# The first batch's v in a chunk-selecting attention with an MLP: six loads by tile of the sequence in place of sixteen by pair of heads

## The chip, the cores and the metric

The kernel runs on one core of a Trainium2 chip. The metric is the device time of one execution in microseconds (us). The kernel before took 303.6 us, the median of three runs (302.7 to 303.85).

## The reference, cut to what matters

For each of 4 batches and 8 heads, 768 queries attend to 768 keys of 64 elements. The keys stand in 24 chunks of 32. An upper bound of each query's score in each chunk is made from the chunk's smallest and largest key elements, the six causal chunks with the highest bounds are kept, and softmax attention runs over those chunks under the causal mask. The heads are then put side by side to rows of 512, and a layer norm, two matrix products (512 to 2048, ReLU, 2048 to 512) and a residual follow.

```python
k_min, k_max = np.min(k_chunks, axis=3), np.max(k_chunks, axis=3)
ub = np.sum(np.maximum(q[:, :, :, None, :] * k_min[:, :, None, :, :],
                       q[:, :, :, None, :] * k_max[:, :, None, :, :]), axis=-1)
ub = np.where(causal, ub, -1000000000.0)
top_chunks = np.argsort(ub, axis=-1)[..., -top_k:]
...
mask = sel & (pos[:, None] >= pos[None, :])
scores = np.where(mask, scale * np.matmul(q, k.transpose(0, 1, 3, 2)), -1000000000.0)
attn = softmax(scores)
x = np.matmul(attn, v).transpose(0, 2, 1, 3).reshape(B, S, H * D)
out = x + np.maximum(layer_norm(x) * g_ln @ w_ch1, 0.0) @ w_ch2
```

## The kernel before, in words

The work unit is a pair of heads of one batch, called g: 4 batches with 4 pairs each give g = 0 to 15. The sequence is cut into 6 tiles of 128 rows, and into two halves r = 0 and 1 of three tiles. The MLP runs by batch b and half r, on 384 rows at a time.

A pair of heads goes through these functions. `load_qk` brings one half of k and of q, two DMAs each, on the queue of SyncE (L195). `turn` transposes them on TensorE (L223), `q_copy` and `k_copy` write them as fp16 into rings of SBUF, `k_bound` takes the chunks' minima and maxima on VectorE (L268, L269) and leaves them in a tile `kc`. `bounds` (L309 to L326), `select` (L339 to L345), `mask_t` (L354) and `mask_ring` (L359) make the mask. `scores` multiplies q by k on TensorE (L411) and takes the exponential on ScalarE (L417), `diag` cuts the triangle on GpSimd (L424), `values` multiplies by v on TensorE (L437), and `normalise` and `pair_stats` finish the rows on VectorE (L446 to L471). The MLP is `centre`, `x_t` (L497), `rstd` (L491, on GpSimd), `mlp1` (L512, 8 matmuls a call) and `mlp2` (L524, 4 matmuls a call: `mlp2(b, r, i, j)` uses the j-th quarter of w2).

v is loaded by `load_v`, and is cast from fp32 to fp16 by the DMA. A tile `va` holds one pair of heads, with a column of ones behind the 64 elements that sums the weights. For the first batch (g = 0 to 3), `load_v(g, i)` brings half i of the sequence with one DMA for each of the two heads (L214: 128 partitions x 3 tiles x 64 elements), and before the first half a memset of the ones on GpSimd (L212). That gives 16 DMAs, 8 for half 0 and 8 for half 1. For the other batches `load_v(g)` brings a whole pair with one DMA of 128 x 12 x 64 (L204).

The weights of the MLP are loaded in four quarters each, `w1_load` and `w2_load`, also as casting DMAs on GpSimd's queue. A copy of one element ahead of each makes the load wait until a given `kc` is there:

```python
    def w2_load(j, g):
        nc.gpsimd.tensor_copy(w2b[0:1, 4 * j, 0:1], st[g]["kc"][0:1, 0, NCH // 2:NCH // 2 + 1])
        nc.gpsimd.dma_start(w2b[:, 4 * j:4 * j + 4, :], w2_r[:, 4 * j:4 * j + 4, :])
```

The order of the work is a list. Every call is a piece with a due time: the first batch's pieces come from a hand-written sequence (`begin`, with the loads that stand in the table `loads`), the others from formulas. A table `MOVED` adds a small shift to the due time of single calls; then the pieces are sorted and called in that order, and a scheduler keeps the order of each engine's queue, with the first batch's instructions tied to each other (L843 to L862). So GpSimd's queue holds, in order: the constants, the 8 loads of v's half 0, triangles and the 4 loads of w1, the 8 loads of v's half 1, one `rstd`, the 4 loads of w2, and the whole-pair loads of v for g = 4, 5 and on, with triangles among them.

GpSimd's DMAs take eight completion semaphores in turn. A DMA waits until the one eight places before it on this queue has landed; SyncE's DMAs have eight of their own.

Of the kernel before, what the change touches and what calls it, by code (L numbers as in the profile page):

```python
# [19 lines left out]
def kernel(  # L20
# [42 lines left out]
    vap = ctx.enter_context(tc.tile_pool(name="vap", bufs=6))  # L63
# [23 lines left out]
    RT = const.tile([P, S], F16, name="RT", tag="RT")  # L87
    tiny = const.tile([1, 1], F32, name="tiny", tag="tiny")
# [23 lines left out]
    def consts_first():  # L112
# [15 lines left out]
        )  # L128
        nc.vector.memset(hsel, 0.0)
# [69 lines left out]
    def load_v(g, i=None):  # L199
        b, hp = divmod(g, HP)  # L200
        if i is None:
            va = st[g]["va"] = vap.tile([P, 2, NT, VW], F16, name="va", tag="va")
            nc.gpsimd.memset(va[:, :, :, D:D + 1], 1.0)
            nc.gpsimd.dma_start(  # L204
                va[:, :, :, 0:D].rearrange("p h t d -> p (h t) d"),
                v[b, 2 * hp:2 * hp + 2].rearrange("h (t p) d -> p (h t) d", p=P),
            )
            return
        a, z = parts(g)[i]
        if not i:  # L210
            st[g]["va"] = vap.tile([P, 2, NT, VW], F16, name="va", tag="va")
            nc.gpsimd.memset(st[g]["va"][:, :, :, D:D + 1], 1.0)  # L212
        for hh in range(2):
            nc.gpsimd.dma_start(  # L214
                st[g]["va"][:, hh, a:z, 0:D],
                v[b, 2 * hp + hh, a * P:z * P].rearrange("(t p) d -> p t d", p=P),
            )
# [211 lines left out]
    def values(g, r):  # L429
        pt, va = st[g]["pt", r], st[g]["va"]  # L430
# [87 lines left out]
    def mlp2(b, r, i, j):  # L518
# [22 lines left out]
        -3: [(load_v, 0, 0), (load_qk, 0, 1), (load_v, 1, 0)],  # L541
        -2: [(load_v, 2, 0), (load_qk, 1, 1)],
        -1: [(load_v, 3, 0), (load_qk, 2, 1)],
        0: [(load_qk, 3, 1), (w1_load, 0, 2)],
        1: [(w1_load, 1, 3)],
        3: [(w1_load, 2, 3), (w1_load, 3, 3), (load_v, 0, 1)],
        4: [(load_v, 1, 1), (load_v, 2, 1), (load_qk, 4, 0)],
        5: [(w2_load, 0, 0), (w2_load, 1, 0), (load_v, 3, 1), (load_qk, 4, 1)],
# [113 lines left out]
    for b in range(B):  # L662
# [14 lines left out]
        if b == 0:  # L677
# [13 lines left out]
            (): -0.04, (0, 1): -0.009, (0, 2): -0.025, (1,): 0.008, (1, 1): 0.017, (1, 2): 0.017,  # L691
            (2,): 0, (2, 4): 0.006, (2, 5): 0.028, (3,): 0, (3, 1): 0.013, (3, 2): 0.013,
            (4,): -0.048, (5,): 0.008, (5, 5): 0.016, (6,): 0.004, (7,): -0.067, (7, 1): -0.07,
            (8,): -0.436, (9,): -0.025, (9, 5): -0.02, (11,): -0.044, (12,): -0.311, (13,): -0.144,
            (14,): -0.138, (14, 5): -0.134, (15,): -0.21, (15, 4): -0.176, (15, 5): 0,
        },
        "centre": {
            (): 0.008, (0,): -0.017, (0, 1): 0, (0, 1, 0): -0.017, (1,): 0, (1, 0, 2): 0.089,
            (1, 1): 0.033, (1, 1, 1): 0.026,
        },  # L700
        "diag": {
            (): -0.046, (0, 0): 0.016, (0, 1): 0.001, (1, 0): 0.012, (1, 1): -0.067, (2,): 0.003,
            (3, 0): -0.003, (3, 1): 0, (4,): -0.056, (6, 0): -0.044, (6, 1): -0.066, (7, 0): -0.178,
            (7, 1): -0.097, (8, 0): -0.399, (8, 1): -0.6, (9, 0): -0.066, (9, 1): -0.069, (11, 0): 0,
            (11, 1): -0.054, (12, 0): -0.04, (12, 1): 0, (13, 0): -0.146, (13, 1): -0.078,
            (14, 0): 0.003, (14, 1): 0, (15, 0): -0.621,
        },
        "k_bound": {
            (0,): -0.011, (1,): -0.011, (2,): -0.009, (3,): -0.018, (4, 0): 0.007, (4, 1): 0.027,
            (5, 1): 0.022, (6, 0): 0.002, (6, 1): 0.107, (7,): -0.058, (8, 0): -0.331,  # L710
            (8, 1): -0.396, (9, 0): 0.002, (9, 1): 0.065, (11, 0): -0.008, (11, 1): 0.025,
            (12, 0): -0.017, (12, 1): -0.015, (13,): -0.032, (14,): 0.028,
        },
        "k_copy": {
            (0,): -0.004, (1, 0): 0.161, (1, 1): 0.063, (2,): 0.006, (3, 0): -0.011, (3, 1): 0.054,
            (4,): 0.024, (5, 0): 0.511, (5, 1): 0.42, (6,): 0.038, (7, 0): -0.032, (9, 1): 0.023,
            (10,): 0.034, (11, 1): 0.026, (12, 0): 0.938, (12, 1): 0.253, (13, 0): 0.002,
            (13, 1): 0.073, (14,): 0.046, (15,): 0.034,
        },
        "k_diag": {  # L720
            (1,): 0.041, (2, 0): 0.13, (3, 0): 0.033, (3, 1): 0.01, (4,): -0.002, (6,): 0.002,
            (7,): -0.058, (8,): -0.331, (9,): -0.138, (10,): -0.023, (11,): 0.02, (12,): 0.006,
            (13,): -0.032, (14,): -0.108, (15,): -0.076,
        },
        "load_qk": {
            (): -0.438, (0, 0): 0.085, (0, 1): -0.538, (1, 0): 0.034, (1, 1): -0.331, (2, 0): 0,
            (2, 1): -0.329, (3, 0): 0.16, (3, 1): -0.169, (4, 0): -0.33, (4, 1): -0.667,
            (5, 0): -0.543, (5, 1): -1.259, (6, 0): 0.011, (6, 1): -0.111, (7, 0): 0.064,
            (7, 1): 0.002, (8, 0): -0.299, (8, 1): -0.593, (10, 0): 0.015, (10, 1): -0.002,
            (11, 0): -0.01, (11, 1): -0.012, (12, 0): 0.082, (12, 1): 0.004, (13, 0): 0.11,  # L730
            (13, 1): 0.159, (14,): 0.026, (15, 0): 0.317, (15, 1): 0.334,
        },
        "load_v": {
            (2,): -0.087, (3, 0): -0.13, (3, 1): -0.568, (4,): -0.551, (5,): -0.547, (6,): -0.163,
            (7,): 0.215, (8,): -0.124, (9,): 0.342, (12,): 0.279, (13,): 0.241, (14,): 0.301,
            (15,): 0.238,
        },
        "mask_ring": {
            (): 0.017, (0, 0): 0.021, (0, 1): 0, (1, 0): 0.036, (1, 1): -0.009, (2, 0): 0.023,
            (2, 1): 0, (4,): 0.064, (5,): 0.074, (6,): 0.076, (7,): 0.016, (8,): -0.257, (9,): 0.076,  # L740
            (10,): 0.209, (11,): 0.066, (12,): 0.08, (13,): 0.102, (14,): 0.139, (15,): 0.093,
        },
        "mask_t": {
            (): -0.004, (0,): 0, (1, 0): -0.019, (1, 1): -0.002, (2,): 0.002, (4,): -0.016,
            (5,): -0.068, (7,): -0.064, (8,): -0.337, (10,): -0.001, (11,): -0.014, (12,): 0.002,
            (13,): -0.082, (14,): 0, (15,): -0.006,
        },
        "mlp1": {
            (0, 0, 2): -0.016, (0, 0, 6): 0.106, (0, 0, 10): 0.098, (0, 0, 14): 0.069,
            (0, 1): -0.023, (0, 1, 0): 0, (0, 1, 2): 0.016, (0, 1, 14): 0.055, (1,): -0.026,  # L750
            (1, 0, 0): 0.016, (1, 0, 2): 0.016, (1, 0, 4): 0.028, (1, 0, 8): -0.014,
            (1, 1, 0): -0.036, (1, 1, 4): -0.178, (1, 1, 10): 0, (1, 1, 14): -0.001, (2,): -0.294,
            (2, 0, 6): -0.616, (2, 0, 12): -0.277, (2, 1, 2): -0.353, (2, 1, 6): -0.28,
            (2, 1, 10): -0.228, (3,): 0.103, (3, 0, 2): 0, (3, 0, 4): 0, (3, 0, 12): 0,
            (3, 0, 14): 0, (3, 1, 0): 0, (3, 1, 4): 0.108, (3, 1, 6): 0, (3, 1, 14): 0.094,
        },
        "mlp2": {
            (): -0.156, (0, 0, 1, 0): -0.071, (0, 0, 1, 3): 0, (0, 0, 2, 0): -0.051, (0, 1): -0.154,
            (0, 1, 0): -0.156, (0, 1, 0, 0): -0.184, (0, 1, 0, 3): -0.145, (0, 1, 1, 0): -0.156,
            (0, 1, 1, 1): 0.152, (0, 1, 2, 0): -0.132, (1,): -0.157, (1, 0, 0, 1): 0,  # L760
            (1, 0, 1, 3): -0.053, (1, 1): -0.138, (1, 1, 0): -0.182, (1, 1, 0, 3): -0.138,
            (1, 1, 2, 2): -0.182, (1, 1, 2, 3): -0.182, (2,): -0.298, (2, 0, 0): -0.323,
            (2, 0, 0, 1): -0.46, (2, 0, 0, 3): -0.305, (2, 0, 1, 0): -0.323, (2, 0, 2, 2): -0.34,
            (2, 0, 2, 3): -0.34, (2, 1): 0, (2, 1, 0, 0): -0.34, (2, 1, 0, 1): -0.18,
            (2, 1, 0, 2): -0.323, (2, 1, 0, 3): -0.298, (2, 1, 1, 0): -0.267, (2, 1, 1, 1): -0.298,
            (2, 1, 1, 2): -0.423, (2, 1, 1, 3): -0.568, (3,): -0.233, (3, 0, 0): 0,
            (3, 0, 0, 2): -0.124, (3, 0, 0, 3): -0.233, (3, 0, 2): -0.332, (3, 1, 0, 0): -0.332,
            (3, 1, 0, 1): -0.374, (3, 1, 1, 1): -0.263, (3, 1, 1, 2): -0.443, (3, 1, 1, 3): -0.009,
            (3, 1, 2, 0): -0.009, (3, 1, 2, 1): 0.115, (3, 1, 2, 2): -0.224, (3, 1, 2, 3): -0.152,
        },  # L770
        "normalise": {
            (1, 0): -0.008, (2,): 0.002, (3,): -0.004, (4, 0): -0.01, (4, 1): -0.002, (6,): 0.002,
            (7,): -0.058, (8,): -0.331, (9,): 0.002, (12,): 0.006, (13,): -0.032, (14, 0): 0.065,
            (14, 1): 0.028,
# [10 lines left out]
            (13, 1): 0.028, (14,): 0.079, (15, 1): -0.015,  # L785
        },
        "q_relu": {
            (4,): -0.097, (5,): 0.065, (6,): 0.052, (7,): 0.041, (8,): -0.224, (9,): 0.084,
            (11,): 0.063, (12,): -0.045, (13,): 0.022,
        },  # L790
        "q_ring": {
# [99 lines left out]
```

## Time and profile before

| what | value |
|---|---|
| runs | 303.6, 302.7 and 303.85 us |
| the profiled execution, its time | 303.4 us |
| its span, first to last instruction | 301.4 us |
| TensorE clock granted | 0.997 of full |
| TensorE's tail, from its last matmul to the end of the span | 4.5 us |
| read from HBM, written to it | 27.27 MB, 6.29 MB |
| packets of GpSimd's DMA queue (q0), of SyncE's (q1) | 29,248 and 60,416 |

A packet here is what one DMA engine moves in one go: one run of 64 elements for q, k and v, one run of 512 elements (1024 bytes as fp16) for the weights. "Landing" is the time from issue to the completion of a DMA. "Idle before" is the idle time of an engine just before a group, with what ended it. A wait names the waiting engine and line, and behind the arrow who released it.

### The profile page before, as it was taken

To read this page: it belongs to the slowest core of one execution; us is meant where nothing else is said; L and a number is where in the kernel's file an instruction comes from. 1 tells how busy PE (TensorE), PEld (TensorE's weight loads), DVE (VectorE), ACT (ScalarE), POOL (GpSimd) and SP (SyncE) were. 2 spreads that over 40 slices of the span, in tenths; PEclk is the share of its full clock that TensorE was granted. 3 is DMA by queue.
4 is the path that set the end of the run, shared out by engine and by line. 5 is a ranking of instruction groups with operands and counts; after the bars stand their busy time and mean duration, and the time that the engine had idled before them with its cause. 6 is when DMAs were issued, how large, how long until landed. Compare 5 with 4: busy or idle time off the path is not lost.

```text
span 301.4 us, 7194 instructions
## 1 busy us (share of the span) xinstructions
PE 288.2 (96%) x2753; PEld 195.4 (65%) x2753; DVE 190.8 (63%) x654; ACT 183.5 (61%) x274; POOL 91.1 (30%) x162
## 2 busy tenths in 40 slices
PE   7887998999999999999999999999999999999993
PEld 3874766765777676777767667766666555555541
DVE  7888655679998788999577768577262282011011
ACT  3983997664788667778665674848368524423310
POOL 9559383152444412733230411223021120000000
PEclk9999999999999999999999999999999999999998
DMA  7999999999659649679572210113010110010111
GB/s 131 208 210 198 180 199 196 164 193 204 149 135 187 124 72 165 110 143 148 88 132 62 78 46 2 41 49 90 35 37 0 37 37 35 35 37 35 70 37 71
DMA packets 90226, 31.41 MB, mean 104 GB/s; under 512 B 78416, under 2 KB 87120, under 8 KB 90192
## 3 DMA queue, kind: packets, MB, share of 16 engines
q1 hardware_dynamic: 60416, 23.61, 33.8%
q0 software_dynamic: 29248, 7.34, 24.8%
q8 instruction: 22, 0.36, 0.5%
q14 instruction: 12, 0.10, 0.1%
q10 hardware_dynamic: 528, 0.00, 0.1%
HBM read 27.27 MB, written 6.29 MB: 111 GB/s over the span
## 4 chain that ended last, share of the span: by engine, by line
PE 75%; DMA 8%; POOL 7%; issue 4%; DVE 4%; ACT 1%; POOLq 0%; ACTq 0%
PE yp L524 24%; PE mm L512 24%; PE mm L411 10%; PE sm L437 6%; PE tr L223 4%; DMA w2b<-in_moe_w_ch_dram 4%; DMA w1b<-in_moe_w_ch_dram 4%; PE ub L326 3%; POOL va L214 2%; PE trh L497 1%; POOL pt L424 1%; PE trh L354 1%; DVE xc L482 1%; ACT pt L417 1%; POOL rstd L491 1%
## 5 line engine op out<-in xcount | busy, mean ns | idle before, releaser
L417 ACT ACTIVATE pt<-mm 128x1024 f16<-128x1024 f32 (+1 forms) x96 | 86.2, 918 | 25.7 <-PE mm L411 25.3
L524 PE MATMUL yp<-w2b,hT 128*128 128x512 f16 x384 | 95.9, 379 | 1.5 <-DMA w2b<-in_moe_w_ch_dram 1.5
L512 PE MATMUL mm<-xT,w1b 128*128 128x384 f16 x512 | 94.3, 326 | 0.0
L516 ACT ACTIVATE hT<-mm 128x768 f16<-128x768 f32 x64 | 51.9, 813 | 49.1 <-PE mm L512 48.8
L512 PEld LDWEIGHTS <-w1b 128*128 128x128 f16 x512 | 48.9, 98 | 29.9 <-issue 0.2
L524 PEld LDWEIGHTS <-hT 128*128 128x128 f16 x384 | 36.4, 98 | 31.8
L424 POOL TENSOR_SCALAR_AFFINE_SELECT pt<-pt 128x768 f16<-128x768 f16 x32 | 28.8, 899 | 89.1 <-ACT pt L417 89.1
L530 DVE SCALAR_TENSOR_TENSOR ot<-yp,rstd,x 128x512 f32<-128x512 f32 x24 | 17.9, 746 | 45.9 <-PE yp L524 45.9
L411 PE MATMUL mm<-QA,KA 128*128 128x128 f16 (+2 forms) x224 | 34.5, 245 | 1.0 <-ACT hT L516 0.5
L411 PE MATMUL mm<-QB,KB 128*128 128x128 f16 (+2 forms) x224 | 34.2, 246 | 0.0
L437 PEld LDWEIGHTS <-pt 128*128 128x128 f16 x672 | 24.6, 98 | 5.6 <-POOL pt L424 1.8
L437 PE MATMUL sm<-va,pt 128*128 128x65 f16 x672 | 26.5, 193 | 1.4 <-POOL pt L424 1.3
L411 PEld LDWEIGHTS <-KA 128*128 128x128 f16 x224 | 17.9, 99 | 8.1 <-issue 2.3
L471 DVE BATCH_NORM_STATS2 bst<-x 128x6 f32<-128x128 f32 x96 | 21.9, 282 | 0.8
L268 DVE TENSOR_REDUCE kc<-tr 128x12 f32<-128x384 f32 x32 | 17.6, 549 | 6.6 <-PE tr L223 4.9
L411 PEld LDWEIGHTS <-KB 128*128 128x128 f16 x224 | 18.0, 98 | 3.5 <-issue 0.8
L446 DVE RECIPROCAL rden<-sm 128x6 f32<-128x6 f32 x32 | 6.1, 191 | 19.7 <-PE sm L437 19.6
L447 DVE TENSOR_TENSOR x<-sm,rden 128x384 f32<-128x384 f32 x32 | 17.8, 557 | 1.0
L223 PE MATMUL tr<-ident_f,qn 128*128 128x128 f32 x96 | 16.2, 278 | 1.3 <-DMA qn<-in_q_dram 1.3
L269 DVE TENSOR_REDUCE kc<-tr 128x12 f32<-128x384 f32 x32 | 17.5, 547 | 0.0
L279 ACT CAST kh<-tr 128x384 f16<-128x384 f32 x24 | 11.6, 484 | 9.2 <-DMA KB<-kh 3.2
L223 PE MATMUL tr<-ident_f,kn 128*128 128x128 f32 x96 | 16.2, 278 | 0.0
(87 smaller groups left out, 354.2 us busy)
## 6 DMA issues: line engine op xcount, KB each, us to landing
kn<-in_k_dram SPq DMA_DIRECT2D x64, 96.0 KB, 3.3
qn<-in_q_dram SPq DMA_DIRECT2D x64, 96.0 KB, 3.7
out_dram<-ot SPq DMA_DIRECT2D x24, 256.0 KB, 2.1
va<-in_v_dram POOLq DMA_DIRECT2D x12, 192.0 KB, 5.5
w1b<-in_moe_w_ch_dram POOLq DMA_DIRECT2D x4, 512.0 KB, 7.7
w2b<-in_moe_w_ch_dram POOLq DMA_DIRECT2D x4, 512.0 KB, 11.2
KA<-kh SPq DMA_DIRECT2D x24, 48.0 KB, 2.1
KB<-kh SPq DMA_DIRECT2D x24, 48.0 KB, 2.0
```

Of the source, the lines that this page charges most:

```text
L223: nc.tensor.transpose(pst[:, t * P:(t + 1) * P], src[:, t], ident_f)
L268: nc.vector.tensor_reduce(kc[:, 0, n], view, axis=AX.X, op=ALU.min)
L411: nc.tensor.matmul(sc[:, hh, o:o + w * P], ks[:, t * P:(t + 1) * P], qs[:, s * P:(s + w) * P], start=True, stop=True,)
L417: nc.scalar.activation(pt[:, n0:n1].rearrange("p n h x -> p h n x"), sc[:, :, 0:o].rearrange("p h (n x) -> p h n x", x=P), ACTF.Exp, scale ...
L424: nc.gpsimd.affine_select(out=dv, in_=dv, compare_op=ALU.is_ge, fill=0.0, base=0, pattern=[[0, 2 * TR], [1, P]], channel_multiplier=-1,)
L437: nc.tensor.matmul(pv[:, hh, s2, :], pt[:, where[t, s], hh, :], va[:, hh, t, 0:D + 1], start=(t == 0), stop=(t == s),)
L447: nc.vector.tensor_tensor(xh(b, r)[:, :, 2 * hp:2 * hp + 2, :].rearrange("p s h d -> p h s d"), pv[:, :, :, 0:D], rden.to_broadcast([P, 2, ...
L471: nc.vector.bn_stats(h["st"][:, i, hp], xh(b, r)[:, i, 2 * hp:2 * hp + 2].rearrange("p h d -> p (h d)"),)
L512: nc.tensor.matmul(hp_[:, i, 0:TR * P], w1b[:, kt, (m + i) * P:(m + i + 1) * P], h["xT"][:, kt], start=(kt == 0), stop=(kt == KT1 - 1),)
L516: nc.scalar.activation(h["hT"][:, m:m + 2], hp_[:, :, 0:TR * P], ACTF.Relu, scale=HS)
L524: nc.tensor.matmul(yp, h["hT"][:, kt, i * P:(i + 1) * P], w2b[:, kt, :], start=(kt == 0), stop=(kt == KT2 - 1),)
L530: nc.vector.scalar_tensor_tensor(ot, yp, h["rstd"][:, i:i + 1], xh(b, r)[:, i].rearrange("p h d -> p (h d)"), op0=ALU.mult, op1=ALU.add,)
```

## The change

v of the first batch gets a tile of its own, `v_first`, for all eight heads and the six tiles of the sequence. `load_v(0, i)` now brings tile i of the sequence for all heads, with one DMA of 128 x 8 x 64. Six calls take the place of 16 DMAs. The ones are set by one memset on VectorE at the start, in place of four on GpSimd. `values` takes its pair out of `v_first` when g is under 4. The pool of `va` has one buffer fewer (5). The table `loads` places the calls: tiles 0 and 1 at step -3, tile 2 at step -2, tile 3 at step 3, tiles 4 and 5 at step 4.

With it the table `MOVED` is another one throughout. On the queues its effects are these. On GpSimd, the whole-pair load of g = 4 (memset and DMA) now stands between the second and the third load of w2, where before all four loads of w2 came first; `w2_load` has entries of its own. On TensorE, all 12 transposes of the first `x_t` stand behind the transposes of q of g = 0, half 1, where before three stood ahead of it and three behind the first matmuls of `mlp1`; further on, calls of `mlp1`, `mlp2`, `scores` and `turn` change places with their neighbours. The number of matmuls of each kind is the same. SyncE's queue has the same order through the first 68 rows of its listing, and swaps a few later.

```diff
-    vap = ctx.enter_context(tc.tile_pool(name="vap", bufs=6))
+    vap = ctx.enter_context(tc.tile_pool(name="vap", bufs=5))
...
+    v_first = const.tile([P, H, NT, VW], F16, name="v_first", tag="v_first")
...
+        nc.vector.memset(v_first[:, :, :, D:D + 1], 1.0)
         nc.vector.memset(hsel, 0.0)
...
-        a, z = parts(g)[i]
-        if not i:
-            st[g]["va"] = vap.tile([P, 2, NT, VW], F16, name="va", tag="va")
-            nc.gpsimd.memset(st[g]["va"][:, :, :, D:D + 1], 1.0)
-        for hh in range(2):
-            nc.gpsimd.dma_start(
-                st[g]["va"][:, hh, a:z, 0:D],
-                v[b, 2 * hp + hh, a * P:z * P].rearrange("(t p) d -> p t d", p=P),
-            )
+        nc.gpsimd.dma_start(v_first[:, :, i, 0:D], v[0, :, i * P:(i + 1) * P].rearrange("h p d -> p h d"))
...
-        pt, va = st[g]["pt", r], st[g]["va"]
+        pt = st[g]["pt", r]
+        va = v_first[:, 2 * g:2 * g + 2] if g < HP else st[g]["va"]
...
-        -3: [(load_v, 0, 0), (load_qk, 0, 1), (load_v, 1, 0)],
-        -2: [(load_v, 2, 0), (load_qk, 1, 1)],
-        -1: [(load_v, 3, 0), (load_qk, 2, 1)],
+        -3: [(load_v, 0, 0), (load_qk, 0, 1), (load_v, 0, 1)],
+        -2: [(load_v, 0, 2), (load_qk, 1, 1)],
+        -1: [(load_qk, 2, 1)],
         0: [(load_qk, 3, 1), (w1_load, 0, 2)],
         1: [(w1_load, 1, 3)],
-        3: [(w1_load, 2, 3), (w1_load, 3, 3), (load_v, 0, 1)],
-        4: [(load_v, 1, 1), (load_v, 2, 1), (load_qk, 4, 0)],
-        5: [(w2_load, 0, 0), (w2_load, 1, 0), (load_v, 3, 1), (load_qk, 4, 1)],
+        3: [(w1_load, 2, 3), (w1_load, 3, 3), (load_v, 0, 3)],
+        4: [(load_v, 0, 4), (load_v, 0, 5), (load_qk, 4, 0)],
+        5: [(w2_load, 0, 0), (w2_load, 1, 0), (load_qk, 4, 1)],
         6: [(w2_load, 2, 1), (w2_load, 3, 1)],
...
         "load_v": {
-            (2,): -0.087, (3, 0): -0.13, (3, 1): -0.568, (4,): -0.551, (5,): -0.547, (6,): -0.163,
...
+            (0, 0): -0.129, (0, 1): -0.083, (4,): -0.551, (5,): -0.582, (6,): -0.163, (7,): 0.215,
...
+        "w2_load": {
+            (0,): 0.265, (1,): 0.256, (2,): 0.189, (3,): 0.183,
+        },
```

## The prediction, made before the changed kernel was run

> **What bounds the kernel now.** I read the busy times first, then the busy time by stage, what TensorE waits for, the chain of waits up to that wait, and last the DMA view of that stage. The page:
>
> ```profile
> PE 288.2 (96%) x2753; PEld 195.4 (65%) x2753; DVE 190.8 (63%) x654; ACT 183.5 (61%) x274; POOL 91.1 (30%) x162
> ```
>
> TensorE is the bound; GpSimd, whose instructions the change removes, is busy for 30%. By stage (span, TensorE busy, and so on):
>
> ```profile
> 0.00:28.00 28.00, 22.72 (x209) 16.97 (x210) 22.45 (x93) 17.65 (x35) 20.14 (x41) 1.00 1.18 187
> 28.00:49.50 21.50, 20.63 (x193) 15.98 (x191) 13.68 (x43) 20.78 (x40) 12.17 (x22) 1.00 1.35 191
> 49.50:53.00 3.50, 1.96 (x11) 0.84 (x10) 1.66 (x11) 1.73 (x2) 1.48 (x2) 1.00 1.22 196
> 53.00:70.00 17.00, 17.00 (x207) 12.37 (x207) 12.72 (x46) 11.67 (x15) 5.31 (x10) 1.00 1.60 189
> ```
>
> TensorE's 13.2 us of idle lie in few places: 5.3 before 28, 0.9 to 49.5, 1.5 to 53, only 1.0 from 53 to 296.9 (0 + 0.58 + 0.46 in the same table), and a tail of 4.5. So after 53 us the end moves by what the start loses or gains. The one long wait near that border, from the view of waits:
>
> ```profile
> PE yp L524 <- DMA w2b<-in_moe_w_ch_dram: 1.5, 1, 1.5
> ```
>
> The ninth matmul of `mlp2` needs the third quarter of w2. The first eight end at 51.42 and it starts at 52.96. The chain of waits into it:
>
> ```profile
> 36.02 0.74 POOL va L214
> ...
> 40.66 12.26 DMA w2b<-in_moe_w_ch_dram
> ...
> 52.96 0.38 PE yp L524
> ```
>
> and GpSimd's timeline ahead of it (start, duration, idle before in brackets):
>
> ```profile
> 25.87 4.64 POOL L214 DMA_DIRECT2D va<-in_v_dram  x6
> 32.34 0.76 POOL L214 DMA_DIRECT2D va<-in_v_dram  x1 [1.82 <-DMA w1b<-in_moe_w_ch_dram]
> 36.02 0.77 POOL L214 DMA_DIRECT2D va<-in_v_dram  x1 [2.93 <-DMA w1b<-in_moe_w_ch_dram]
> ```
>
> Read alone, this says that eight loads of v keep GpSimd until 36.8 and w2 goes out late. The DMA view for 28 to 53 us says otherwise (packets, MB, share of 16 engines), as do the times to landing, each asked in a window of its own: second and third quarter of w2, then v of g = 4 and of g = 5:
>
> ```profile
> q0 software_dynamic: 6054, 3.23, 92.0%
> q1 hardware_dynamic: 6098, 1.50, 40.5%
> ```
>
> ```profile
> w2b<-in_moe_w_ch_dram POOLq DMA_DIRECT2D x1, 512.0 KB, 10.1
> ...
> w2b<-in_moe_w_ch_dram POOLq DMA_DIRECT2D x1, 512.0 KB, 12.3
> ...
> va<-in_v_dram POOLq DMA_DIRECT2D x1, 192.0 KB, 17.4
> ...
> va<-in_v_dram POOLq DMA_DIRECT2D x1, 192.0 KB, 18.0
> ```
>
> GpSimd's DMA queue (q0) is backlogged throughout. Issue plus landing gives one file: w1's last quarter 35.7, the eight loads of v 36.7 to 42.3, w2's quarters 46.2, 49.5, 53.0 and 56.2, then v of g = 4 at 60.1, g = 5 at 62.6. From one to the next: 6.6 us for v's 3,072 packets, 3.9 for the first quarter, 3.3 for each later one, 3.9 and 2.5 for 1,536 packets of v. What comes when depends on the place in this file, not on when GpSimd issues.
>
> [...]
>
> **The change part by part.**
>
> *Issues and memsets.* 16 issues x 0.772 us (median of L214) and 4 memsets x 0.169 leave GpSimd: 13.0 us. Six issues come. Their cost isn't shown; per DMA it lies between 0.77 (384 packets) and 1.06 (1,536, L204), for 1,024 packets I take 0.92 by the straight line, 5.5 in all. In the first half 3.9 us are saved (6.7 - 2.8), but after its constants GpSimd waits until 14.77 for ScalarE's exponential (3.16 us), so they vanish. In the second half the saving reaches only the issue of w2, which queues behind the same packets. Worth 0.
>
> *Packets.* v has 3,072 packets per half before and after. What a run of 8 heads in place of 3 tiles does to a packet is not shown: I take the same 6.6 us, and 5.0 as the low bound, twice the pace of g = 5.
>
> *First half of v.* Its first use is at 16.77 us. Before, the last of the 8 DMAs landed at 14.8 (issue 9.95, 4.8 to landing). Now three are issued by about 7 us, so they aren't later unless each packet is slower. They meet the loads of q and k that TensorE waits for (0.7 us at 7.25, 0.6 at 10.5). From 5 to 14 us q0 moved 3,197 packets, already behind its issues, so q and k lose 0 to 0.5 us. Whatever moves before 49 us is swallowed by the wait for w2 anyway.
>
> *The memset on VectorE* delays the start by 0.06 to 0.33 us (the memsets of L129 and L136), taken as 0.1; *the transposes of `x_t`* behind those of q may win the 0.3 and 0.16 us of idle on L497. Both end in the same wait: 0.
>
> *Eight semaphores.* Before, the last two loads of v waited for w1 (1.8 and 2.9 us). With ten DMAs fewer the loads of half 1 wait for old loads only; the third and fourth load of w2 wait for w1's last two quarters (about 32 and 36 us). Queued behind them on GpSimd is the triangle of g = 0, half 1, run at 43.7: not late. Worth 0 while the queue is backlogged.
>
> *v of g = 4 ahead of w2's third quarter.* This is the step that costs. On GpSimd it is a memset (0.17) and an issue (1.04), hidden. In the file it is 1,536 packets: 3.9 us by its own landing, 2.5 by that of g = 5; I take 3.2. So w2's third quarter lands at 53.0 + 3.2 = 56.2 where TensorE wants it at about 51.4. TensorE waits 4.7 us in place of 1.5. [...] The fourth quarter is as late (59.4), and its first user moves from 59.78 to about 63: no second wait.
>
> *The rest of `MOVED`.* The matmuls are the same, and from 53 us on TensorE has 1.0 us of idle to lose: -0.5 to +1, taken as 0.
>
> *Sum.* 303.4 (the profiled execution: span 301.4 and 2.0 around it) + 3.2 = 306.6. The median of the runs is 303.6, 0.2 above it, within their spread. Own range: +2.5 - 0.5 to +3.9 + 1, so 305.4 to 308.3[...].
>
> **The rivals.** *The eight heads pack better.* If v runs at the pace of g = 5, half 1 takes 5.0 in place of 6.6 and g = 4 takes 2.5: +0.9, so 304.3, no change that can be measured. For it: g = 5 to 7 landed 2.5 to 2.8 us apart. Against it: v of g = 4, with runs of 12, took 3.9.
>
> *The chain of waits is right, and the wait goes.* The other side: GpSimd is free at 28.7 in place of 36.8, w2 goes out some 8 us earlier, and if the file moves with the issues the wait of 1.5 us at L524 ends: 303.4 - 1.5 = 301.9, and no more, since the remaining idle isn't touched. It decides once w2's third quarter lands before 51.4, which with g = 4 ahead of it needs 4.8 us out of the file. Against it: landings every 3.3 us with no gap.
>
> *The new order costs by itself*, without w2: TensorE gets new gaps after 53 us, by 2 us or more: 305.5. For it: VectorE and ScalarE are busy for 9.4 and 9.1 of 10 us around 80 to 90. Against it: the order there changes by neighbours only.
>
> **How the numbers follow.** Forecast 0.58, better packing 0.21, the wait gone 0.15, new order 0.06. About 0.5% (1.5 us) is what a measurement can tell from no change here. The first and last are slower by more; the second is within; the third is faster: 0.64, 0.21, 0.15. The range runs from 302.2, which cuts off most of the third, to 308.6, which takes in the forecast's high end.
>
> **What would show it.** Right: the idle before L524 at w2 grows to 4 to 5.5 us, v of g = 4 lands before w2's third quarter, and busy TensorE time stays at 288. Wrong: that wait is under 2 us; or w2's third quarter lands by 52; or GpSimd's earlier freedom shows in landings before 45 us. Wrong too: a wait on `va` or on q in the first 28 us that reaches past 50.

## The result, and the profile after

The changed kernel takes 311.13 us (median, 310.61 to 312.94), the kernel before beside it 303.55 us: a ratio of 1.0265, 95% interval 1.0218 to 1.0312. That is 7.6 us slower, where 3 were predicted, and above the predicted range (302.2 to 308.6). The profiled execution took 310.83 us, its span is 308.8 (before: 303.4 and 301.4).

The page of the kernel after, busy times and granted clock:

```profile
PE 293.7 (95%) x2753; PEld 199.9 (65%) x2753; DVE 191.2 (62%) x655; ACT 184.0 (60%) x274; POOL 83.4 (27%) x148
...
PEclk9959999999999999999999999999999999999999
```

TensorE runs the same 2,753 matmuls but is busy 5.5 us longer. The work is the same, so the clock must have fallen, and the digit 5 in the third slice of `PEclk` says where: about 15 to 23 us. The stages (span, TensorE busy, ..., and third from the end the granted clock):

```profile
0.00:28.00 28.00, 23.33 (x169) 18.74 (x170) 17.30 (x76) 16.21 (x33) 11.66 (x24) 0.82 1.01 162
28.00:49.50 21.50, 18.46 (x160) 13.40 (x158) 15.02 (x54) 15.77 (x30) 12.28 (x22) 1.00 1.34 184
49.50:53.00 3.50, 3.43 (x28) 2.63 (x27) 1.39 (x5) 3.46 (x7) 3.50 (x7) 1.00 1.45 172
53.00:70.00 17.00, 15.55 (x176) 10.87 (x176) 10.83 (x39) 11.85 (x17) 3.54 (x7) 1.00 1.54 178
```

By 28 us, 169 matmuls are done in place of 209, in more busy time. The loss is at the very start, not near 53 us. TensorE's timeline there shows what came ahead of the clock's fall; first after, then before:

```profile
9.99 0.52 PE L218 MATMUL tr<-ident_f,kn 128*128 128x128 f32 x3 [0.26 <-DMA kn<-in_k_dram]
12.55 0.52 PE L218 MATMUL tr<-ident_f,qn 128*128 128x128 f32 x3 [2.04 <-DMA qn<-in_q_dram]
```

```profile
10.50 0.52 PE L223 MATMUL tr<-ident_f,qn 128*128 128x128 f32 x3 [0.62 <-DMA qn<-in_q_dram]
```

The transposes of q of g = 2 start 2.05 us later, after a wait of 2.04 us in place of 0.62. Then the clock, in stretches cut at its changes:

```profile
10.54:13.95 3.41, 1.40 (x15) 1.39 (x15) 2.02 (x7) 1.68 (x5) 0.00 (x0) 1.00 1.35 213
13.95:24.19 10.24, 10.24 (x71) 9.34 (x71) 4.40 (x22) 7.16 (x14) 2.78 (x5) 0.50 0.83 153
24.19:28.00 3.81, 3.41 (x49) 2.76 (x48) 3.19 (x15) 1.89 (x3) 1.62 (x2) 1.00 1.24 218
```

For 10.24 us TensorE works without a gap at a granted clock of 0.50, which by that share costs 5.1 us. The delay of 2.05 and these 5.1 make 7.2; some small waits vanish, and the first matmul of `mlp1` starts at 34.84 us in place of 28.38: +6.5.

Why was q late? SyncE issued it at the same time in both kernels: its last DMA goes out at 6.61 us, but takes 5.81 us to land (chain of waits, after) in place of 3.8 (DMA view, before):

```profile
6.61 5.81 DMA qn<-in_q_dram
```

```profile
qn<-in_q_dram SPq DMA_DIRECT2D x1, 96.0 KB, 3.8
```

So it was the transfer that took longer. Packets of GpSimd's queue (q0, here v) and of SyncE's (q1, q and k) from 7 to 11 us, after and then before:

```profile
q0 software_dynamic: 2468, 0.31, 121.1%
q1 hardware_dynamic: 1434, 0.35, 55.0%
```

```profile
q0 software_dynamic: 1629, 0.20, 79.3%
q1 hardware_dynamic: 2380, 0.58, 75.5%
```

The sum is the same (3,902 and 4,009), but v moved 839 more packets and q and k 946 fewer. GpSimd issued v's 3,072 packets within 2.9 us (4.22 to 7.1) in place of 6.5 us (4.22 to 10.73). After, then before:

```profile
4.22 2.88 POOL L212 DMA_DIRECT2D v_first<-in_v_dram  x3
```

```profile
4.22 1.75 POOL L214 DMA_DIRECT2D va<-in_v_dram  x2
...
9.19 1.55 POOL L214 DMA_DIRECT2D va<-in_v_dram  x2
```

By 7.1 us GpSimd's queue had moved 298 packets, before the change 475. An estimate from these numbers: some 2,800 packets of v were issued and not yet moved at that moment, against 700 to 1,100 before.

And the step that was forecast? The chain of waits and the waits at w2's third quarter:

```profile
39.83 19.43 DMA w2b<-in_moe_w_ch_dram
59.30 0.38 PE yp L520
```

```profile
PE yp L520 <- DMA w2b<-in_moe_w_ch_dram: 1.3, 1, 1.3
```

v of g = 4, issued at 38.34, lands 17.8 us later, at 56.1, and w2's third quarter at 59.3: v of g = 4 does stand ahead of it. But TensorE waits 1.3 us, not 4.7, since it was itself 6.5 us late. The ninth matmul of `mlp2` starts at 59.30 in place of 52.96, +6.3; the remaining 1.1 of the 7.4 us by which the span grew come later.

### The profile page after: what moved, and what is told of

The parts are those of the page before. It is cut to its first block, busy times and chain, and to the rows that moved or that the text cites. A ratio compares the mean times of both kernels' runs of the same rounds, so it can differ in the third digit from the quotient of the medians.

```text
span 308.8 us, 7189 instructions
## 1 busy us (share of the span) xinstructions
PE 293.7 (95%) x2753; PEld 199.9 (65%) x2753; DVE 191.2 (62%) x655; ACT 184.0 (60%) x274; POOL 83.4 (27%) x148
## 4 chain that ended last, share of the span: by engine, by line
PE 70%; DVE 12%; DMA 10%; issue 2%; ACT 2%; SPq 2%; POOL 1%; ACTq 0%; DVEq 0%
PE yp L520 24%; PE mm L508 20%; PE mm L406 9%; DMA w2b<-in_moe_w_ch_dram 6%; PE sm L433 5%; PE tr L218 4%; DMA qn<-in_q_dram 3%; PE ub L321 3%; SPq L197 2%; PE ub L311 2%; PE trh L493 1%; DVE xc L478 1%; DVE kc L263 1%; DVE bst L467 1%; DVE kc L264 1%
## 5 line engine op out<-in xcount | busy, mean ns | idle before, releaser
L412 ACT ACTIVATE pt<-mm 128x1024 f16<-128x1024 f32 (+2 forms) x96 | 86.1, 920 | 24.7 <-PE mm L406 24.5
L419 POOL TENSOR_SCALAR_AFFINE_SELECT pt<-pt 128x768 f16<-128x768 f16 x32 | 27.9, 871 | 100.0 <-ACT pt L412 99.8
L406 PE MATMUL mm<-QB,KB 128*128 128x128 f16 (+2 forms) x224 | 35.0, 250 | 0.0
L406 PEld LDWEIGHTS <-KA 128*128 128x128 f16 x224 | 18.8, 102 | 7.8 <-issue 1.8
L218 PE MATMUL tr<-ident_f,qn 128*128 128x128 f32 x96 | 17.2, 286 | 2.4 <-DMA qn<-in_q_dram 2.0
L433 PE MATMUL sm<-va,pt 128*128 128x65 f16 x504 | 19.4, 193 | 0.0
L443 DVE TENSOR_TENSOR x<-sm,rden 128x384 f32<-128x384 f32 x32 | 17.8, 555 | 0.9
L497 ACT ACTIVATE xT<-trh,gstr 128x384 f16<-128x384 f16 x16 | 9.2, 580 | 14.2 <-PE trh L493 14.0
L218 PE MATMUL tr<-ident_f,kn 128*128 128x128 f32 x96 | 16.9, 288 | 0.3 <-DMA kn<-in_k_dram 0.3
```

Of the source, the lines that this page charges most:

```text
L218: nc.tensor.transpose(pst[:, t * P:(t + 1) * P], src[:, t], ident_f)
L406: nc.tensor.matmul(sc[:, hh, o:o + w * P], ks[:, t * P:(t + 1) * P], qs[:, s * P:(s + w) * P], start=True, stop=True,)
L412: nc.scalar.activation(pt[:, n0:n1].rearrange("p n h x -> p h n x"), sc[:, :, 0:o].rearrange("p h (n x) -> p h n x", x=P), ACTF.Exp, scale ...
L419: nc.gpsimd.affine_select(out=dv, in_=dv, compare_op=ALU.is_ge, fill=0.0, base=0, pattern=[[0, 2 * TR], [1, P]], channel_multiplier=-1,)
L433: nc.tensor.matmul(pv[:, hh, s2, :], pt[:, where[t, s], hh, :], va[:, hh, t, 0:D + 1], start=(t == 0), stop=(t == s),)
```

## The experiments

Two theories stood at first. *Clock*: v's fast issue takes the DMA engines from q, the wait halves TensorE's clock. *Order*: the new table `MOVED` costs by itself. The place of v of g = 4, the prediction's reason, was a third. "Old table" and "new table" are `MOVED` of before and after.

**e1, the six loads alone**: the changed kernel with the old table.

> The six loads of v alone, with the old table of shifts (so v of g = 4 stands behind all four loads of w2). Clock theory (v's first three DMAs take the DMA engines from q, TensorE stands 2 us at the transposes of q of g = 2, and its clock halves for 10 us): the wait and the halved clock are both there, the first mlp1 matmul starts near 34.8 us in place of 28.4, w2's third quarter is no longer late, and the time is 308 to 309.8. Order theory (the new table costs the 7 us): full clock, 303 to 304.5. File theory (only v of g = 4 ahead of w2's third quarter costs): 303.4 also, but with the old wait of 1.5 us at w2 unchanged.

307.49 us (305.47 to 307.77), ratio 1.0128 [1.0084, 1.0172]. The wait on q is 2.12 us, the granted clock is 0.50 from 13.89 to 24.13, the first `mlp1` is at 34.76, and TensorE doesn't wait for w2. The clock theory holds for the loads, and its time came out a little low. The loads alone don't make the 7.6 us, though.

**e2, the table alone**: the kernel before with the new table; in the part on `load_v` only the entry of g = 5 is the new one, so the 16 loads stay in place.

> The new table of shifts alone, with the 16 loads of v at their old places (v of g = 4 stands between the second and third load of w2, as in the changed kernel). Clock theory: no long wait on q, clock full from 6 us on; the wait at w2's third quarter grows from 1.5 to about 4.7 us and the time is 306 to 307, as the prediction had it. Order theory: 310 to 311. If the place of v of g = 4 is worth nothing: 303.4.

310.52 us (310.13 to 311.17), ratio 1.0248 [1.0209, 1.0286]: the number of the order theory, which I had not believed. The view of waits, and the busy times around the wait:

```profile
PE yp L524 <- DMA w2b<-in_moe_w_ch_dram: 4.3, 1, 4.3
```

```profile
49.50:54.74 5.24, 2.08 (x12) 0.95 (x10) 2.32 (x13) 1.89 (x2) 1.64 (x2) 1.00 1.34 186
54.74:61.57 6.83, 5.66 (x24) 3.59 (x24) 2.23 (x5) 2.18 (x3) 0.00 (x0) 0.50 1.50 179
```

The predicted wait is there, 4.3 us with w2 at 55.9 (predicted: 4.7 and 56.2). What was not in the sum is the second line: 6.83 us at a granted clock of 0.50 after it.

**e3, v behind k**: the changed kernel, with each of v's first three loads made to wait for a `kc` (and their two shifts dropped).

```diff
+        if i < 3:
+            nc.gpsimd.tensor_copy(v_first[0:1, 0, i, 0:1], st[i]["kc"][0:1, 0, 0:1])
         nc.gpsimd.dma_start(v_first[:, :, i, 0:D], ...)
...
-        -3: [(load_v, 0, 0), (load_qk, 0, 1), (load_v, 0, 1)],
-        -2: [(load_v, 0, 2), (load_qk, 1, 1)],
-        -1: [(load_qk, 2, 1)],
+        -3: [(load_v, 0, 0), (load_qk, 0, 1)],
+        -2: [(load_v, 0, 1), (load_qk, 1, 1)],
+        -1: [(load_v, 0, 2), (load_qk, 2, 1)],
```

> The changed kernel, but each of the first three loads of v waits for a chunk minimum (kc of g = 0, 1, 2), by a copy of one element ahead of it, so that q and k of half 0 go first. Clock theory: the wait on q of g = 2 falls from 2.0 us to under 0.8, the clock stays full, first mlp1 near 28.5 to 29.5; then v of g = 4 in the file shows and TensorE waits 4 to 5 us at w2's third quarter: 306 to 307.5. A wait on v at the first values up to 1 us may come, and be swallowed by the wait for w2. Order theory: 310 or more, as the table is unchanged. Rival to the clock theory (shape of the loads or the memset on VectorE slows the start): first mlp1 still after 33, 309 or more.

309.73 us (307.68 to 310.72), ratio 1.0208 [1.0159, 1.0256]. Its view of waits, and the DMA in its chain of waits that leads to w2's third quarter (start, duration):

```profile
PE yp L522 <- DMA w2b<-in_moe_w_ch_dram: 4.2, 1, 4.2
...
PE tr L220 <- DMA qn<-in_q_dram: 0.8, 1, 0.8
```

```profile
33.85 22.33 DMA w2b<-in_moe_w_ch_dram
```

With v held back the long wait on q is gone, the granted clock is 1.00 up to 56.8 us and the first `mlp1` is at 28.88. Then the w2 wait comes up at its full 4.2 us, with 3.42 us at 0.50 behind it. The expected time was too low by that clock. The chain also shows w2's third quarter issued at 33.85 and landing at 56.2. In e2, with the same loads ahead of it in the queue, it was issued at 40.99 and landed at 55.9: 7.1 us of earlier issue brought no earlier landing.

**e4, the wait on q filled**: 18 matmuls of 240 columns, unused, ahead of the transposes of q of g = 2.

```diff
+            if new == (2, 0):
+                begin += [(fill, 18)]
             if done != (HP - 1, 0):
                 begin += [(turn, g, "qn", i)]
```

> The changed kernel with 18 extra matmuls of 240 columns (results unused) on TensorE just before the transposes of q of g = 2: they fill the 2 us for which TensorE waited, about 1.9 us of work, and leave the DMAs as they are. Clock theory: the clock stays full though q comes as late as before, the first mlp1 starts near 30.2 (28.4 + 1.8) in place of 34.8, and the wait for w2's third quarter grows to 3 to 5 us; 306 to 307.5. If the wait itself and not the clock carries the cost, or the clock has another cause: clock again half from 14 to 24 us, first mlp1 near 34.8, 310.5 to 311.5.

310.83 us (309.34 to 311.66), ratio 1.0247 [1.0203, 1.0291]. The time alone would speak against the clock theory; the trace doesn't. The granted clock is 1.00 up to 49.5 us, though q of g = 2 lands nearly as late as in the changed kernel (12.2 and 12.4 us), and the first wait no longer costs more than its filling. Then TensorE waits 3.7 us for w2 and has some 3.4 us of half clock (an estimate from the granted 0.86 between 49.5 and 60 us and 0.98 between 60 and 70). As with e3, one loss was taken away and the other came out from under it. From here on the theory was: **two waits, each of which halves the clock when it is met in full** (2.04 us on q in the changed kernel, 4.3 us at w2 in e2). In the changed kernel the first makes TensorE so late that only 1.3 us of the second are left, and no half clock follows them.

**e5, both waits removed**: e3 with the whole-pair loads of v of g = 4 and 5 behind all of w2 (`(4,): -0.2, (5,): -0.19` in `load_v`).

> The gated kernel of e3 (first three loads of v wait for kc), and in addition the whole-pair loads of v of g = 4 and 5 put behind all four loads of w2; the table of shifts is otherwise the new one. Theory of two waits (the q wait at 12 us and the w2 wait at 52 us each halve TensorE's clock; all else of the change costs about 1 us): the wait at w2's third quarter falls to 1 to 2 us, the clock is full from start to end, 303.3 to 305. Order theory (the new table costs by itself, beyond the place of g = 4): 307 or more with the clock full.

303.94 us (303.45 to 306.34), ratio 1.0040 [1.0022, 1.0058]. The granted clock is 1.00 up to 297 us, and the wait at w2 is 1.2 us. All else of the change, the copies that hold v back included, costs about 1.2 us by the ratio, 0.7 by the medians.

**e12, only g = 4 put back**: the changed kernel with those two entries alone.

> The changed kernel with the whole-pair loads of v of g = 4 and 5 behind all four loads of w2, nothing else changed. Theory of two waits: the wait on q and the half clock from 14 to 24 us stay, the wait at w2's third quarter (1.3 us) goes, 308 to 309.8. If the place of g = 4 carried the loss: 303.5 to 305.

308.69 us (308.0 to 309.34), ratio 1.0190 [1.0160, 1.0220]. The wait on q (2.06 us) and the half clock after it (0.50 from 13.12 to 19.94 us) stay; the wait for w2 is gone.

So the four corners are: neither wait 303.9 (e5), q alone 308.7 (e12), w2 alone 309.7 (e3), both 311.1 (the changed kernel). Alone they cost 4.8 and 5.8, together 7.2. (In e3 and e5 the copies that hold v back are included, in the other two they are not.)

**e11, the w2 wait filled**: e2 with 40 unused matmuls ahead of the matmuls that wait.

```diff
     def mask_t(g, i=None):
+        if (g, i) == (2, 1):
+            junk = ps_m.tile([P, 2, 512], F32, name="fill", tag="mm")
+            for _ in range(40):
+                nc.tensor.matmul(junk[:, 0, 0:240], ident_b, ...)
...
```

(A further line ties the waiting call of `mlp2` behind the filling.)

> e2 (new table, old loads) with 40 extra matmuls of 240 columns, 4.2 us of work with unused results, ahead of the matmuls that wait for w2's third quarter; mask_t and what follows it come after the filling. TensorE loses about the same 4.2 us there as in e2, but busy. If the half clock after the wait is the part that the prediction left out: full clock, 306 to 307, the number predicted. If the clock is a by-product and the wait itself with the new table makes the 7 us: 309.5 to 311.

307.28 us (306.69 to 309.98), ratio 1.0156 [1.0109, 1.0204]. The filling and the stretch around it:

```profile
50.56 4.26 PE L358 MATMUL fill<-causb,ident_b 128*128 128x240 bf16 x40
```

```profile
49.50:60.00 10.50, 10.50 (x99) 8.71 (x97) 5.59 (x20) 5.23 (x7) 1.88 (x3) 1.00 1.38 182
```

As many microseconds are lost at the same place, but busy, and the granted clock stays at 1.00: 3.2 us less than e2. By an estimate from e2's second line the half clock accounts for 2.8 of them: in its 6.83 us at 0.50 TensorE was busy for 5.66, and at 1.00 half of these would have done. (The slowest of e11's four executions, 309.98 us, was granted 0.989 of the clock, the others 0.996 to 0.998.)

**Shape or pace?** Both start from e1. e6 loads half 0 of v with the old eight DMAs; e7 keeps the three new ones and puts four memsets between them.

```diff
+    def load_vh(hp):
+        for h in range(2 * hp, 2 * hp + 2):
+            nc.gpsimd.dma_start(v_first[:, h, 0:TR, 0:D], v[0, h, 0:TR * P].rearrange("(t p) d -> p t d", p=P))
```

```diff
         nc.gpsimd.dma_start(v_first[:, :, i, 0:D], ...)
+        if i < 2:
+            for _ in range(4):
+                nc.gpsimd.memset(causf, 0.0)
```

> e1 (six loads, old table), but half 0 of v goes into the new tile by the old eight DMAs of 128 x 3 x 64, at their old places; half 1 stays with three DMAs of 128 x 8 x 64, and the memset of the ones stays on VectorE. If three DMAs issued in 2.9 us, or their runs of eight heads, take q's share: no wait of over 0.8 us on q, full clock, first mlp1 near 28.5, 303 to 304. If the memset on VectorE or the smaller pool delays the start: the wait and the half clock stay, 307 to 308.

> e1 (six loads, old table), but with four memsets of the causal constant (overwritten later) on GpSimd after the first and after the second load of v, so that the three DMAs go out about 2.3 us apart, at the pace in packets of the old eight, with their new shape. If the fast issue (a deeper backlog on GpSimd's queue) gives v its larger share: the wait on q of g = 2 falls under 0.9 us, full clock, 303 to 304.5. If the shape (eight heads side by side in a DMA) does it: packets of v still outnumber those of q and k from 7 to 11 us, the wait stays at 1.5 us or more, the clock halves, 306.5 to 308.

e6: 302.74 us (302.26 to 304.59), ratio 0.9995 [0.9984, 1.0006]. e7: 303.75 us (302.45 to 305.07), ratio 1.0012 [0.9992, 1.0032]. Packets of e7 from 7 to 11 us:

```profile
q0 software_dynamic: 1720, 0.22, 84.0%
q1 hardware_dynamic: 2280, 0.56, 77.4%
```

With the new shape at the old pace, v's share is nearly the old one (before: 1,629 to 2,380) and the wait on q is 0.41 us. Here it is the pace of issue, not the eight heads side by side. e6, where the memset on VectorE and the smaller pool stay, clears those two.

**e9 and e10, a part of the wait filled**: e1 with 9 or 4 unused matmuls at the place of e4. The question of both: does the clock fall at some length of the wait, which e10 calls the threshold, or does the cost shrink in proportion to the wait?

> e1 (six loads, old table) with 9 extra matmuls of 240 columns before the transposes of q of g = 2: about 0.95 us of the 2.1 us wait is filled, 1.2 us of idle stays and q comes as late as before. [...] full clock, first mlp1 near 30.3, the delay of 1.9 us ends partly in the old wait for w2, 303.6 to 304.6. If the cost of the wait shrinks in proportion: half the stretch at half clock, 305 to 306.

> The same with 4 extra matmuls, 0.42 us, so that 1.7 us of idle stays. It only tells where the threshold lies: above 1.7 us the clock stays full and the time is 303.6 to 304.6; below, TensorE goes at half clock for about 10 us as in e1 and the time is 306.5 to 308.

e9: 304.99 us (304.51 to 305.65), ratio 1.0065 [1.0043, 1.0087], a granted clock of 1.00 up to 297 us with 1.11 us of idle left ahead of q of g = 2; slightly above what was expected, since q of g = 1 was waited for too (1.04 us). e10: median 306.39, but twelve executions from 303.28 to 309.12. Its runs can only be read with their clocks: four had 0.996 to 1.000 and 303.3 to 304.8 us, four 0.982 to 0.986 and 306.2 to 307.3, four 0.974 to 0.975 and 308.7 to 309.1. The profiled one is of the first kind, with 1.51 us of idle. So in e10 the cost isn't in proportion to the wait: it comes at three levels, near 304.0, 306.7 and 308.9 us by the middles of these ranges, in executions of one and the same kernel. Why one execution takes one and not another isn't shown.

**e8, a version made from this**: the kernel before, with half 1 of v of the pairs 2 and 3 behind the fourth load of w2.

```diff
-        4: [(load_v, 1, 1), (load_v, 2, 1), (load_qk, 4, 0)],
-        5: [(w2_load, 0, 0), (w2_load, 1, 0), (load_v, 3, 1), (load_qk, 4, 1)],
-        6: [(w2_load, 2, 1), (w2_load, 3, 1)],
+        4: [(load_v, 1, 1), (load_qk, 4, 0)],
+        5: [(w2_load, 0, 0), (w2_load, 1, 0), (load_qk, 4, 1)],
+        6: [(w2_load, 2, 1), (w2_load, 3, 1), (load_v, 2, 1), (load_v, 3, 1)],
```

(The shifts of those two calls are set to 0.)

> The kernel before, with half 1 of v of the pairs 2 and 3 (four DMAs, first used at 61.5 us) put behind the fourth load of w2. If landings follow the file: w2's quarters land 3.3 us earlier, the third at about 49.7, TensorE no longer waits 1.5 us for it, the end moves by 1.5: 301.4 to 302.2. If the wait is replaced by another (v of g = 2, half 1, or v of g = 4, late): 303 to 305.

302.33 us (301.8 to 304.83), ratio 0.9973 [0.9955, 0.9992]: the fastest of all, but by 0.8 us and not by the 1.5 that were expected. The profiled span is 300.0. The wait for w2 is gone and none takes its place (kernel before, then e8):

```profile
49.50:60.00 10.50, 8.96 (x94) 6.48 (x93) 6.61 (x28) 6.02 (x8) 2.41 (x4) 1.00 1.50 174
```

```profile
49.50:60.00 10.50, 10.50 (x106) 7.49 (x105) 7.69 (x30) 7.41 (x10) 4.37 (x8) 1.00 1.68 161
```

The tiles of the change forbid this: there, tile 5 of all heads is one DMA, and `values(0, 1)` needs it at once.

## Why the prediction was wrong, point by point

- *First half of v*: **the step that failed.** It said "q and k lose 0 to 0.5 us" and "Whatever moves before 49 us is swallowed by the wait for w2 anyway". q of g = 2 was 2.05 us later, since v issued in 2.9 us takes 63% of the packets from 7 to 11 us (e7: 43% when it is spaced). The step looked at when the last load of v is issued, and not at their pace: by the estimate above some 2,800 packets of v were pending at 7.1 us, against 700 to 1,100 before. Nor was it swallowed: the half clock, to which this step gave no term, made it 6.5 us against a wait of 1.5. And the wait moves along: the loads of w1 and w2 are held by `kc`, which TensorE's transposes feed, so w1's third quarter went out at 30.0 in place of 23.9 and w2's third quarter, with v of g = 4 ahead of it besides, landed 6.3 us later. That the change is slower was forecast, but for the most part this is another loss than the one forecast: with the forecast step taken out (e12) the kernel still takes 308.7 us.
- *v of g = 4 ahead of w2's third quarter*: mechanism and size right where it is seen alone (e2: third quarter 2.9 us later where 3.2 were taken, 4.3 us of wait for 4.7; e11: 4.1 us slower than the kernel before beside it, 3.2 forecast). In the changed kernel it is mostly hidden, 1.3 us. Even alone the sum would have failed by the half clock, for which it had no term: e3 has 3.42 us of it, which by the granted 0.50 cost 1.7, and e2 6.83 us, which cost 2.8 by the estimate (3.2 between the times of e2 and e11). The trace of the kernel before has one such fall, in its tail: the last matmul ends at 296.84 us and the granted clock is 0.50 from 299.31 on, 2.5 us later, where it costs nothing (the last digit of its `PEclk` is 8).
- *Issues and memsets*: the new issue takes 0.96 us (2.88 for three), 0.92 was taken. "Worth 0" is right for the gain: e3 issues w2's third quarter 7.1 us earlier than e2 and lands it no earlier. But the time freed on GpSimd wasn't neutral: it is what made the issue fast.
- *Packets*: w2's third quarter lands at 52.2 in e7, which has the new shape in both halves, and at 51.7 in e6, which has it in the second; before, at 52.9. The new shape wasn't slower there; that it packs better isn't shown by 0.7 to 1.2 us in one profile each.
- *The memset on VectorE*: the first wait of TensorE for VectorE is 1.5 in place of 1.3 us; 0.1 was taken. *The transposes of `x_t`*: still 0.5 on ScalarE, 0.7 on `xc`; nothing won, as said. *Eight semaphores*: 0, and the waits of 1.8 and 2.9 us did vanish. (In both traces GpSimd's DMAs carry the semaphores 111 to 118 in turn, and SyncE's eight others.)
- *The rest of `MOVED`*: taken as 0, with +1 as its end; e5 leaves about 1.2 us, the held-back loads included. From 100 to 200 us TensorE is idle for 0.72 us in the changed kernel, 0.29 in the kernel before.
- "Busy TensorE stays at 288": it was 293.7, the sign that settled the reading.
- The rivals: better packing isn't shown (see the packets); the wait didn't go through earlier issues (e3); and the new order alone was slow (e2), but by the wait and the clock (e11), not through gaps after 53 us. The warning "a wait on `va` or on q in the first 28 us that reaches past 50" named what happened, and had no time or chance in the sum.

## What to carry to other kernels

Where fewer and larger DMAs free the issuing engine, look at what that raises: here v's 3,072 packets were issued in 2.9 us in place of 6.5, and those pending at 7.1 us rose to some 2,800, by the estimate above. Ask which other queue's loads are due in those few microseconds, and hold the ones that aren't urgent. Price a wait of TensorE with the clock that follows it: here waits of 2.0 to 4.3 us had 3.4 to 10.24 us of half clock behind them, and the wait of 1.5 us in the kernel before had none. When taking away one loss moves the time little, look in the trace for the next loss that came out from under it, and remove both before judging either.

## What the runs showed of the hardware that was not expected

- **The clock fell after waits of 2 us.** The prediction's sum had no term for it. Waits of 2.04 us (the changed kernel), 2.06 (e12), 2.12 (e1), 3.7 (e4), 4.2 (e3) and 4.3 us (e2) had half clock behind them; the wait of 1.5 us in the kernel before had none, and e10, whose profiled execution waits 1.51 us at a granted 1.00, came out with a mean clock of 0.974 to 1.000 from one execution to the next.
- **How busy TensorE was just before a fall.** In the changed kernel it worked for 1.40 of the 3.41 us before the fall at 13.95 us and for 0.17 of the 3.41 before the one at 307.49, where the last matmul ends; in the kernel before, for 0.95 of the 3.42 before the fall at 299.31, in its tail. With the wait for w2 in it, the stretch from 50.13 to 53.54 us of the kernel before holds 1.87 us of work, and the granted clock stays at 1.00. These are counts from two traces; what decides the fall isn't shown, and no run was made to try it.
- **The length of the fall.** The half clock lasted 3.42 us in e3, 6.83 in e2, 6.82 in e12's profiled execution and 10.24 in e1 and the changed kernel. 2.0 us of idle came before 10.24 us of it in the changed kernel and before 6.82 in e12; 4.3 us before 6.83 (e2), 4.2 and 3.7 us before 3.4 (e3, e4). In these runs it doesn't follow the length of the wait. Nor does it follow the busy time: TensorE was busy throughout in the half clock of e1, e3, e12 and the changed kernel. What sets the length isn't shown.
- **Two DMA queues didn't share evenly.** From 28 to 53 us of the kernel before they moved as many packets each (6,054 and 6,098); from 7 to 11 us packets of v to those of q and k stood 1.72 to 1 when v was issued fast (2,468 to 1,434), 0.75 to 1 when spaced (e7: 1,720 to 2,280), at nearly the same sum (3,902 and 4,000). Equal numbers alone wouldn't show that the queues compete; that from the kernel before to the changed one v gains 839 while q and k lose 946 does. e7 changes only the pace of issue, so the pace is shown to be the cause here. That the number of pending packets is what matters is an inference, and why it would was not tried.
